# Six of the seven second products of a Winograd pair: w2's columns as weights, tokens moving, sums turned on VectorE

## The chip, the core and the metric

The program runs on one core of a Trainium2 chip. TensorE (PE in the profile; its weight loads are PEld) multiplies, VectorE (DVE) and ScalarE (ACT) do elementwise work, GpSimd (POOL) and SyncE (SP) mostly start DMAs. Matmuls write PSUM, of which this kernel uses eight banks of 128 partitions x 512 floats. The metric is the device time of one execution in microseconds, the median of several runs.

## The reference, cut to what matters

One transformer block for 2048 tokens of width 512: a modulated layer norm, linear attention and a residual, then a second modulated layer norm, a dense layer to 1792 features, Mish, and a dense layer back to 512, again with a gate and a residual:

```python
h = _layernorm(x) * (1 + cb) + sb
sp = softplus(h @ w1 + b1);  act = (h @ w1 + b1) * tanh(sp)      # Mish, [2048, 1792]
x = x + gb * (act @ w2)                                           # w2: [1792, 512]
```

All is float32. The kernel carries each operand as two float32r parts (hi, lo) and takes hi x hi, hi x lo and lo x hi: three matmuls stand for one product (`mm3`, L72).

## The kernel before

**Blocks and tiles.** The tokens are four blocks of 512; the 1792 features are 14 tiles of 128 (`NF`), taken in seven pairs (`G`). Blocks 0 and 1 go through the feed-forward layer first: the first dense layer as a Winograd scheme of seven products per pair (`product`, `pair_begin`, `pair_early`, `pair_middle`, `pair_end`, L1127 to L1184), the second one plainly (`d_unit`, L1107), with the activations as weights, 128 tokens at a time, and 512 columns of w2 moving.

**The last two blocks** (2 and 3; from L1305) use a Winograd scheme for the second layer too. Its left matrix has the two blocks as rows and the two feature tiles of a pair as columns (a11, a12 of block 2, a21, a22 of block 3); its right matrix has the two feature tiles as rows and the two halves of w2's 512 columns as columns. Per pair there are seven products, each summed over the seven pairs in PSUM: m1 = a11 b11, m2 = a12 b21, m4 = a22 t4, m5 = s1 t1, m6 = s2 t2, m7 = s3 t3, m3 = s4 b22. The left sums are s1 = a21 + a22, s2 = s1 - a11, s3 = a11 - a21 (in the code a21 - a11, taken with a sign), s4 = a12 - s2. The results are m1 + m2, m1 + m6 + m5 + m3, m1 + m6 + m7 - m4 and m1 + m6 + m7 + m5, each plus a residual that lies in DRAM (`x1d`).

**One unit** is one product of one pair: `seventh` (L1321) with four tiles of 128 tokens as weights, three matmuls each, 256 columns of w2's part moving: 12 matmuls. The two PSUM banks of a product hold two token tiles of 256 columns each. m1 and m2 are run between the products of the first layer (`e_unit`, `gap`, L1333 and L1416; for the last pair after the second unit of m4), then come m4, m6, m7, m5 as 28 units in this order (L1435 to L1461). m3 (L1463 to L1471) comes last and by token tiles: 21 matmuls of 256 columns, an add, a store, four times.

**Order of the work.** It is written out by hand: each engine runs its instructions in the order in which the code emits them. Work beside TensorE's is kept in generators, which `tick` (L57) moves on by one step after each unit; `spawn` puts one in line, `spawn_idle` into a second line of which a few move on per tick. `left_sums` (L1337) makes the left sums in place, `split` makes hi on ACT and lo on DVE, `left_prep` (L1355) prepares a left operand some five units ahead. `left_trail` does it for the first five pairs during the first layer. `finish` (L1361) adds a finished product into the residual tiles `rq`, 512 elements per partition at a time, and stores them; `load_r` (L1310) loads these tiles from DRAM on SP.

**Buffers.** Tiles of 2 KB per partition come from one pool of `SLOTS` = 97; whoever needs a tile takes the one that has been free longest and waits for its last reader. A DMA that loads weights (`load_wb` L763, `load_wt` L1388, on POOL) or residuals (SP) so waits for a tile.

**w2's preparation** (`w2_job`, L702) runs during blocks 0 and 1: each 128 rows of w2 are multiplied with the gate on DVE, split, and written to DRAM; `w2_sums` (L730) makes the four right sums of a pair.

Of the kernel before, what the change touches and what calls it, by code (L numbers as in the profile page):

```python
# [13 lines left out]
P = 128  # L14
S = 2048
D = 512
# [1 line left out]
NB = S // 512  # L18
NF = F // P
LAG = 3  # L20
SLOTS = 97
EPS = 1e-5
TINY = 1e-6

# [1 line left out]
def block_kernel(ctx: ExitStack, tc: tile.TileContext, x, wqkv, wo, w1, b1t, w2, c, wmodt, out):  # L26
# [668 lines left out]

    w2r = {}

    def load_w2(f):
        w2r[f] = sb(f"w2r_{f}")
        sp.dma_start(w2r[f], w2[P * f:P * (f + 1), :])  # L700

    def w2_job(f, wait=2):  # L702
        if f not in w2r:
            load_w2(f)
            for _ in range(wait):
                yield
        t = w2r[f]
        dve.tensor_tensor(t, t, bc["gb"], op=ALU.mult)
        yield
        yield from split(f"w2_{f}", t, w2s, f)  # L710
        yield
        g, n = f // 2, f % 2
        if n == 0:
            if g in SUMS_KEPT:
                w2f[g] = drp.tile([P, 2, D], F32, name=f"w2f_{g}")
            for i in range(2):
                w2d[g, i] = drp.tile([P, 2, D], F32R, name=f"w2d_{g}_{i}")
        for i in range(2):
            pool.dma_start(w2d[g, i][:, n, :], w2s[f][i])
        if g in SUMS_KEPT:  # L720
            pool.dma_start(w2f[g][:, n, :], t)
        elif g < KEPT and n:
            for _ in range(1 if g else 6):
                yield
            yield from w2_sums(g)
# [4 lines left out]
    def w2_sums(g):  # L730

        if g in SUMS_KEPT:
            r = [sb(f"w2p_{g}_{i}") for i in range(2)]
            for i in range(2):
                sp.dma_start(r[i], w2f[g][:, i, :])
        else:
            r = [w2r[2 * g + i] for i in range(2)]
        yield
        yield
        h = D // 2  # L740
        b11, b12, b21, b22 = [v[:, c:c + h] for v in r for c in (0, h)]
        ta, tb = [sb(f"t{n}_{g}") for n in (12, 34)]
        t1, t2, t3, t4 = ta[:, 0:h], ta[:, h:D], tb[:, 0:h], tb[:, h:D]
# [158 lines left out]
    def o_post(p, b, t):  # L902
        r = xt["r", b, t]
        dve.tensor_tensor(r, p, r, op=ALU.add)  # L904
        if b >= 2:
            yield
            if t % 2 == 0:
                x1d[b, t // 2] = drp.tile([P, 2, D], F32, name=f"x1d_{b}_{t // 2}")
            pool.dma_start(x1d[b, t // 2][:, t % 2, :], r)

    def o_unit(b, t, tag="acc"):
        p = ps(tag, f"o_{b}_{t}")
# [206 lines left out]

    ub = {}  # L1120
# [186 lines left out]
    banks, rq, U = {}, {}, {}  # L1307
    width[0] = 3

    def load_r(n, c):  # L1310

        for i in range(2):
            rq[n, c, i] = sb(f"rq_{n}_{c}_{i}", F32, (P, 2, D // 2))
            sp.dma_start(rq[n, c, i], x1d[L + n, i][:, :, D // 2 * c:D // 2 * (c + 1)])

    def store(n, c, i, lo=0, hi=2):
        r0 = 512 * (L + n) + 2 * P * i
        sp.dma_start(out[r0 + P * lo:r0 + P * hi, D // 2 * c:D // 2 * (c + 1)].rearrange("(t p) c -> p t c", p=P),
                     rq[n, c, i][:, lo:hi, :])

    def seventh(name, tag, left, right, n, last):  # L1321

        if n == 0:
            banks[name] = [ps(tag, f"{name}_{i}") for i in range(2)]
# [5 lines left out]
    def bank(name, i):  # L1330
        return banks[name][i].rearrange("p (t c) -> p t c", t=2)

    def e_unit(c, n):  # L1333
        g = pairs[n]
# [2 lines left out]
    def left_sums(g, fine=False):  # L1337

        a11, a12, a21, a22 = ua[2 * g], ua[2 * g + 1], ub[2 * g], ub[2 * g + 1]
        yield from split(f"l4_{g}", a22, left, ("m4", g))  # L1340
        for n, (d, u, v, op) in enumerate(((a22, a21, a22, ALU.add), (a21, a11, a21, ALU.subtract),
                                           (a11, a22, a11, ALU.subtract), (a12, a12, a11, ALU.subtract))):
            if fine or n == 2:
                yield
            dve.tensor_tensor(d, u, v, op=op)
        sums_of[g] = {"m5": a22, "m7": a21, "m6": a11, "m3": a12}

    left, sums_of = {}, {}

# [3 lines left out]
        yield from left_sums(g, True)  # L1353

    def left_prep(name, g):  # L1355
        return left_sums(g) if name == "m4" else split(f"l_{name}_{g}", sums_of[g][name], left, (name, g))

    def add_r(n, c, i, v, op=ALU.add):
        dve.tensor_tensor(rq[n, c, i], rq[n, c, i], v, op=op)

    def finish(name):  # L1361
        for i in range(2):
            p = bank(name, i)
            if name == "m2":
                U[i] = sb(f"U_{i}", F32, (P, 2, D // 2))
                act.activation(U[i], bank("m1", i), AF.Copy)
                add_r(0, 0, i, bank("m1", i))
                add_r(0, 0, i, p)
                store(0, 0, i)
            if name == "m4":  # L1370
                add_r(1, 0, i, p, ALU.subtract)
            if name == "m6":
                dve.tensor_tensor(U[i], U[i], p, op=ALU.add)
                add_r(0, 1, i, U[i])
            if name == "m7":
                dve.tensor_tensor(U[i], U[i], p, op=ALU.add)
                add_r(1, 0, i, U[i])
                store(1, 0, i)
                add_r(1, 1, i, U[i])
            if name == "m5":  # L1380
                add_r(0, 1, i, p)
                add_r(1, 1, i, p)
                store(1, 1, i)
            yield

    wt, SUM = {}, {"m5": 0, "m6": 1, "m7": 2, "m4": 3}

# [14 lines left out]
    for n, g in enumerate(pairs):  # L1402
# [9 lines left out]
            load_r(0, 0)  # L1412
        if n == 6:
            for m in pairs[:5]:
                load_wt("m4", m)
        def gap(c, m):  # L1416
            def unit():
                e_unit(c, m)
# [21 lines left out]
    load_r(1, 0)  # L1440
    tags = {"m4": "h", "m6": "acc", "m7": "acc", "m5": "h"}
    for k, (name, n) in enumerate(units[:4 * G]):
        for _ in range(2 if k in (6, 10, 14, 18) else 1):
            if ahead_of:
                nm, m = ahead_of.pop(0)
                spawn(left_prep(nm, pairs[m]))
        for _ in range(2 if k < 3 else 1):
            if loads:
                nm, m = loads.pop(0)
                load_wt(nm, pairs[m])  # L1450
        if k in (3, 8):
            load_r(k // 8, 1)
        seventh(name, tags[name], left.pop((name, pairs[n])), wt.pop((name, pairs[n])), n, G - 1)
        if n == G - 1:
            spawn(finish(name))
        tick()
        if k == 1:
            e_unit(0, G - 1)
            e_unit(1, G - 1)
            spawn(finish("m2"))  # L1460
            tick()  # L1461

    last = [ps("acc", f"m3_{t}") for t in range(4)]  # L1463
    for t in range(4):
        p = last[t][:, 0:D // 2]
# [3 lines left out]
        v = rq[0, 1, t // 2][:, t % 2, :]  # L1469
        dve.tensor_tensor(v, v, p, op=ALU.add)  # L1470
        store(0, 1, t // 2, t % 2, t % 2 + 1)  # L1471


# [30 lines left out]
```

## Time and profile before

| what | us |
| --- | --- |
| runs | 489.94, 490.17, 492.12 (median 490.17) |
| the profiled execution, its own time | 490.62 |
| its span in the profile | 488.9 |
| TensorE busy in it | 482.3 (99%), 2574 matmuls |
| VectorE, ScalarE, GpSimd busy | 397.8, 303.9, 120.5 |
| first layer of the last two blocks, with m1 and m2 | 348.19 to 432.21 |
| m4, the last of m1 and m2, m6, m7, m5 | 432.21 to 475.44 |
| m3 and the end | 475.44 to 488.9 |

In the order of time, a row has the start in us, the duration in us, the engine, the line, the operation, what it writes and from what, the shapes, and in brackets how long the engine sat idle before it and what ended that. Matmuls overlap: the time that one takes in a stream is the distance of two starts, not the duration. In the rows of a stretch, each engine has its busy time and its instructions in brackets; behind them stand the granted clock of TensorE, the busy share of the DMA engines and GB/s. In rows of a tile or a line, the durations are least/median/most in ns. Rows of DMA issues give KB of each and us to landing. Tile names have their numbers left out: `m` is the PSUM tile of any of m1 to m7, `p_a` and `p_s` those of the first layer.

### The profile page before, as it was taken

How to read it: one execution, taken by the hardware profiler on the slowest of the kernel's cores; microseconds unless marked ns; L12 is line 12 of the kernel's file. 1: busy time of each engine (PE TensorE's matmuls, PEld its weight loads, DVE VectorE, ACT ScalarE, POOL GpSimd, SP SyncE). 2: the span in 40 equal slices, each digit the busy share in tenths (PEclk: the TensorE clock that was granted, in tenths of full speed). 3: DMA queues.
4: the chain of work that ended last, by engine and by line, in shares of the span. 5: the costliest groups of instructions: out<-in, count | busy, mean ns of one | idle time of the engine just before them, and what ended most of it. 6: DMA issues, size and time to landing. Idle time of an engine off the chain costs nothing.

```text
span 488.9 us, 7482 instructions
## 1 busy us (share of the span) xinstructions
PE 482.3 (99%) x2574; PEld 404.5 (83%) x2574; DVE 397.8 (81%) x775; ACT 303.9 (62%) x549; POOL 120.5 (25%) x200
## 2 busy tenths in 40 slices
PE   8999999999999999999999999999999999999997
PEld 6688877768887888888888888888888888899997
DVE  6999898998999799988998763798444898869772
ACT  6787469755754979557887655783065576668100
POOL 3673121000022123113435115141101100445200
PEclk9999999999999999999999999999999999999999
DMA  8904859644884428168759359994733304688612
GB/s 303 379 8 88 193 109 275 198 130 117 263 203 110 108 68 255 65 195 279 241 164 252 120 138 293 370 341 108 215 87 86 88 0 130 156 214 233 154 44 86
DMA packets 67392, 83.88 MB, mean 172 GB/s; under 512 B 6001, under 2 KB 41337, under 8 KB 67354
## 3 DMA queue, kind: packets, MB, share of 16 engines
q1 hardware_dynamic: 44424, 48.65, 33.1%
q0 software_dynamic: 22784, 34.49, 26.5%
q8 instruction: 20, 0.33, 0.3%
q10 hardware_dynamic: 146, 0.26, 0.1%
q14 instruction: 18, 0.15, 0.1%
HBM read 56.89 MB, written 24.38 MB: 166 GB/s over the span
## 4 chain that ended last, share of the span: by engine, by line
PE 84%; DMA 6%; DVE 6%; ACT 1%; SPq 1%; POOL 1%; issue 1%; DVEq 0%
PE p_a L1133 20%; PE p_s L1133 8%; PE oacc L76 5%; PE oacc L75 5%; PE oacc L74 5%; PE m L76 5%; PE m L75 5%; PE m L74 5%; PE o L74 3%; PE o L76 3%; PE o L75 3%; PE pq_a L376 3%; DMA sq_x<-wide_x 3%; DMA wm<-in_wmodt_dram 2%; PE pq L74 2%; PE pq L76 1%
## 5 line engine op out<-in xcount | busy, mean ns | idle before, releaser
L1143 ACT ACTIVATE u<-p_a 128x512 f32<-128x512 f32 x14 | 8.4, 598 | 29.2 <-PE p_a L1133 29.2
L767 POOL DMA_DIRECT2D wb<-w2d x14 | 9.8, 705 | 67.2 <-PE p_a L1133 30.6
L1138 DVE TENSOR_TENSOR cb<-p_s,u 128x512 f32<-128x512 f32 x28 | 19.1, 686 | 7.7 <-ACT u L1174 7.6
L199 POOL TENSOR_TENSOR rs_n<-rs_n,half 128x1 f32<-128x1 f32 x16 | 10.0, 627 | 57.1 <-DVE rs_n L225 44.3
L1125 ACT ACTIVATE ub<-cb,b1c 128x512 f32<-128x512 f32 x28 | 20.0, 718 | 5.6 <-DVE cb L1138 5.5
L1168 ACT ACTIVATE u<-p_a 128x512 f32<-128x512 f32 x12 | 7.2, 598 | 25.8 <-PE p_a L1133 25.8
L1400 POOL DMA_DIRECT2D wt_m<-w2t x20 | 14.0, 702 | 29.1 <-PE m L76 20.9
L880 POOL DMA_DIRECT2D rden_d<-rden x2 | 1.5, 736 | 60.3 <-DVE rden L878 60.3
L1102 ACT ACTIVATE u<-p_a,b1c 128x512 f32<-128x512 f32 x14 | 9.6, 688 | 9.6 <-PE p_a L1133 9.6
L773 POOL DMA_DIRECT2D w2b<-w2d x20 | 10.6, 543 | 20.0 <-PE oacc L76 12.4
L1138 DVE TENSOR_TENSOR c<-p_a,u 128x512 f32<-128x512 f32 x14 | 9.5, 685 | 6.4 <-PE p_a L1133 5.2
L1174 ACT ACTIVATE u<-p_a 128x512 f32<-128x512 f32 x14 | 8.3, 595 | 8.7 <-PE p_a L1133 8.3
L1117 DVE TENSOR_TENSOR r<-oacc,r 128x512 f32<-128x512 f32 x8 | 5.5, 691 | 8.8 <-PE oacc L76 8.8
L290 DVE SCALAR_TENSOR_TENSOR ku<-e_k,relu_k 128x512 f32<-128x512 f32 x16 | 11.3, 703 | 1.5 <-ACT relu_k L288 1.5
L290 DVE SCALAR_TENSOR_TENSOR q<-e_q,relu_q 128x512 f32<-128x512 f32 x16 | 10.6, 683 | 1.2 <-ACT relu_q L288 1.2
L199 POOL TENSOR_TENSOR rs_x<-rs_x,half 128x1 f32<-128x1 f32 (+1 forms) x10 | 7.8, 786 | 15.0 <-DVE rs_x L194 14.2
L190 DVE BATCH_NORM_STATS2 st_x<-x 128x6 f32<-128x512 f32 x13 | 8.8, 676 | 3.1 <-DMA x<-in_x_dram 3.1
L904 DVE TENSOR_TENSOR r<-o,r 128x512 f32<-128x512 f32 x16 | 10.8, 675 | 0.6 <-PE o L76 0.6
L287 ACT ACTIVATE e_k<-pk 128x512 f32<-128x512 f32 x16 | 9.4, 586 | 2.7 <-PE pk L76 2.7
L892 DVE SCALAR_TENSOR_TENSOR q<-q,rd 128x512 f32<-128x512 f32 x16 | 10.4, 683 | 0.2 <-DMA rd<-rden_d 0.2
L299 POOL DMA_DIRECT2D ku<-ku x8 | 7.2, 939 | 13.4 <-DVE ku L290 13.4
L175 DVE SCALAR_TENSOR_TENSOR wm<-wm,sc_row 128x512 f32<-128x512 f32 x16 | 10.4, 680 | 0.0
(1588 smaller groups left out, 1981.7 us busy)
## 6 DMA issues: line engine op xcount, KB each, us to landing
wm<-in_wmodt_dram SPq DMA_DIRECT2D x24, 256.0 KB, 5.4
w1p<-in_w_dram SPq DMA_DIRECT2D x24, 256.0 KB, 5.3
w2b<-w2d POOLq DMA_DIRECT2D x20, 256.0 KB, 7.9
wt_m<-w2t POOLq DMA_DIRECT2D x20, 256.0 KB, 4.5
r<-in_x_dram SPq DMA_DIRECT2D x16, 256.0 KB, 2.8
x<-in_x_dram SPq DMA_DIRECT2D x15, 256.0 KB, 4.8
w2r<-in_w_dram SPq DMA_DIRECT2D x14, 256.0 KB, 5.7
wb<-w2d POOLq DMA_DIRECT2D x14, 256.0 KB, 3.6
```

Of the source, the lines that this page charges most:

```text
L74: pe.matmul(o, st[0], mv[0], start=start, stop=False)
L75: pe.matmul(o, st[0], mv[1], start=False, stop=False)
L76: pe.matmul(o, st[1], mv[0], start=False, stop=stop)
L199: pool.tensor_tensor(y, y, half[:, lo:hi], op=ALU.pow)
L290: dve.scalar_tensor_tensor(dst, e, 1.0, r, op0=ALU.min, op1=ALU.add)
L376: pe.matmul(p, l, r, start=onto is None and c == 0 and i == 0, stop=c == 1 and i == 2, skip_group_check=onto is not None)
L773: pool.dma_start(w2s[f][i], w2d[f // 2, i][:, f % 2, :])
L904: dve.tensor_tensor(r, p, r, op=ALU.add)
L1125: act.activation(u, p, AF.Mish, bias=b1c[:, f:f + 1])
L1133: pe.matmul(p, st, mv, start=onto is None and c == 0 and i == 0, stop=c == 1 and i == 2, skip_group_check=onto is not None)
L1138: dve.tensor_tensor(out, p, u, op=ALU.add)
L1400: pool.dma_start(v, w2t[g][:, :, SUM[name], :])
```

## The change

For all products but m3, the roles are turned. The weights are now 128 columns of w2's part (its 256 columns in two groups q), and the left operand's 512 tokens move: two groups, three matmuls each, 6 matmuls of 512 columns per unit. A product's two banks now hold w2's columns on the partitions and 512 tokens in a row. m3 keeps its form.

So the sums come out turned. `total` adds two parts into a tile `y` and turns it in blocks of 32 x 32 on VectorE into one large tile `z` (two groups, two results at a time). For that the first half of w2's columns is kept in another order: column 64a + 32q + c lies at 128q + 32a + c, so that a partition of `z` has 64 columns, 256 bytes, that lie together in the output. `w2_job` writes this order when it multiplies with the gate, in two instructions per tile and into a new tile; `w2_sums` reads the second half in the same order; blocks 0 and 1 undo it in their last add, also in two instructions.

The residual of a result is loaded in the same pieces (`load_r`: four DMAs of 32 partitions, 16 x 256 bytes each) into one buffer `Y`, added in one instruction of 1024 elements (`result`), and stored in such pieces (`store`), on SP or ACT. One result, m1 + m6 + m5 of block 2's second half, goes to DRAM (`c12`) and is loaded back as rows (`rn`), and m3 is added to it. The order of the products becomes m6, m5, m7, m4, m3; s1 gets a tile of its own, since a22 is needed until m4. The pool has 95 tiles.

```diff
-SLOTS = 97
+SLOTS = 95
...
-        t = w2r[f]
-        dve.tensor_tensor(t, t, bc["gb"], op=ALU.mult)
+        v, t = w2r[f], sb(f"w2g_{f}")
+        for h, d in enumerate(halves(t)):
+            c = slice(D // 2 * h, D // 2 * (h + 1))
+            s_ = [u[:, c] if h else u[:, c].rearrange("p (a q c) -> p a q c", a=4, q=2) for u in (v, bc["gb"])]
+            dve.tensor_tensor(d, *s_, op=ALU.mult)
+        w2r[f] = t
...
-                dve.tensor_tensor(v, oacc[t], v, op=ALU.add)
+                h0 = v[:, 0:D // 2].rearrange("p (a q c) -> p a q c", a=4, q=2)
+                dve.tensor_tensor(h0, halves(oacc[t])[0], h0, op=ALU.add)
+                dve.tensor_tensor(v[:, D // 2:D], oacc[t][:, D // 2:D], v[:, D // 2:D], op=ALU.add)
...
+    def in_squares(d, c):
+        return [bass.AP(tensor=d.tensor, offset=d.offset + H * c + 64 * a, ap=[[D, 32], [32 * D, 16], [1, 64]])
+                for a in range(4)]
     def load_r(n, c):
-        for i in range(2):
-            rq[n, c, i] = sb(f"rq_{n}_{c}_{i}", F32, (P, 2, D // 2))
-            sp.dma_start(rq[n, c, i], x1d[L + n, i][:, :, D // 2 * c:D // 2 * (c + 1)])
+        y = rq[n, c] = big.tile([P, 16, 64], F32, tag="Y", name=f"rq_{n}_{c}", bufs=1)
+        for a, d in enumerate(in_squares(x1d[L + n], c)):
+            sp.dma_start(y[32 * a:32 * (a + 1)], d)
+    def store(n, c, y, d=None, eng=sp):
+        if d is None:
+            d = out[512 * (L + n):512 * (L + n + 1), :]
+        for a, v in enumerate(in_squares(d, c)):
+            eng.dma_start(v, y[32 * a:32 * (a + 1)])
     def seventh(name, tag, left, right, n, last):
...
-        for t in range(4):
-            h = t % 2
-            mm3(banks[name][t // 2][:, D // 2 * h:D // 2 * (h + 1)], [a[:, P * t:P * (t + 1)] for a in left], right,
-                n == 0 and h == 0, n == last and h == 1)
+        for q in range(2):
+            mm3(banks[name][q], [w[:, P * q:P * (q + 1)] for w in right], left, n == 0, n == last)
...
+    def total(n, c, q, u, p, op=ALU.add):
+        y = sb(f"y_{n}_{c}_{q}")
+        dve.tensor_tensor(y, u, p, op=op)
+        if not Z:
+            Z.append(big.tile([P, 16, 4, 32], F32, tag="W", name="z", bufs=1))
+        dve.transpose(Z[0][:, :, 2 * (n ^ c) + q, :], y.rearrange("p (m c) -> p m c", c=32))
+    def result(n, c):
+        z = Z[0][:, :, 2 * (n ^ c):2 * (n ^ c) + 2, :].rearrange("p m q c -> p m (q c)")
+        dve.tensor_tensor(z, z, rq.pop((n, c)), op=ALU.add)
+        if (n, c) != (0, 1):
+            store(n, c, z, eng=sp if c == n else act)
+            return
+        d = drp.tile([512, D], F32, name="c12")
+        store(n, c, z, d)
+        for i in range(2):
+            rn[i] = sb(f"rn_{i}", F32, (P, 2, H))
+            sp.dma_start(rn[i], bass.AP(tensor=d.tensor, offset=d.offset + 2 * P * D * i + H,
+                                        ap=[[D, P], [P * D, 2], [1, H]]))
...
-    names = ["m4", "m6", "m7", "m5", "m3"]
+    names = ["m6", "m5", "m7", "m4", "m3"]
...
-        if k in (3, 8):
-            load_r(k // 8, 1)
+        if k in (2, 10, 17):
+            load_r(*{2: (0, 1), 10: (1, 1), 17: (1, 0)}[k])
```

`finish` now does, for q = 0 and 1 one tick apart: after m2 a copy of m1 to `U` on ACT and the total U + m2; after m6 U + m6; after m5 a copy of m5 to `V` on ACT and the total U + m5; after m7 U + m7 and the total U + V; after m4 the total U - m4. `result` follows one tick later (three after m2).

More of the change, by code (lines that the diff above doesn't have):

```diff
@@ L906, in o_post @@
             yield
-            if t % 2 == 0:
-                x1d[b, t // 2] = drp.tile([P, 2, D], F32, name=f"x1d_{b}_{t // 2}")
-            pool.dma_start(x1d[b, t // 2][:, t % 2, :], r)
+            if t == 0:
+                x1d[b] = drp.tile([4, P, D], F32, name=f"x1d_{b}")
+            pool.dma_start(x1d[b][t], r)
     def o_unit(b, t, tag="acc"):
@@ L1339, in left_sums @@
         a11, a12, a21, a22 = ua[2 * g], ua[2 * g + 1], ub[2 * g], ub[2 * g + 1]
-        yield from split(f"l4_{g}", a22, left, ("m4", g))
-        for n, (d, u, v, op) in enumerate(((a22, a21, a22, ALU.add), (a21, a11, a21, ALU.subtract),
-                                           (a11, a22, a11, ALU.subtract), (a12, a12, a11, ALU.subtract))):
+        s1 = sb(f"ls_{g}")
+        for n, (d, u, v, op) in enumerate(((s1, a21, a22, ALU.add), (a21, a11, a21, ALU.subtract),
+                                           (a11, s1, a11, ALU.subtract), (a12, a12, a11, ALU.subtract))):
             if fine or n == 2:
@@ L1345, in left_sums @@
             dve.tensor_tensor(d, u, v, op=op)
-        sums_of[g] = {"m5": a22, "m7": a21, "m6": a11, "m3": a12}
+        sums_of[g] = {"m4": a22, "m5": s1, "m7": a21, "m6": a11, "m3": a12}
+        yield from split(f"l_m6_{g}", a11, left, ("m6", g))
     left, sums_of = {}, {}
@@ L1361, in finish @@
     def finish(name):
-        for i in range(2):
-            p = bank(name, i)
+        for q in range(2):
+            p = banks[name][q]
             if name == "m2":
[L1365 to L1369, printed above, removed]
-            if name == "m4":
[L1371 to L1383, printed above, removed]
-            yield
+                U[q] = sb(f"U_{q}")
+                act.activation(U[q], banks["m1"][q], AF.Copy)
+                total(0, 0, q, U[q], p)
+            if name == "m6":
+                dve.tensor_tensor(U[q], U[q], p, op=ALU.add)
+            if name == "m5":
+                V[q] = sb(f"V_{q}")
+                act.activation(V[q], p, AF.Copy)
+                total(0, 1, q, U[q], p)
+            if name == "m7":
+                dve.tensor_tensor(U[q], U[q], p, op=ALU.add)
+                total(1, 1, q, U[q], V[q])
+            if name == "m4":
+                total(1, 0, q, U[q], p, ALU.subtract)
+            yield
@@ L1386, in block_kernel @@
+        if name != "m6":
+            if name == "m2":
+                yield
+                yield
+            result(*{"m2": (0, 0), "m5": (0, 1), "m7": (1, 1), "m4": (1, 0)}[name])
     wt, SUM = {}, {"m5": 0, "m6": 1, "m7": 2, "m4": 3}
@@ L1468, in block_kernel @@
         tick()
-        v = rq[0, 1, t // 2][:, t % 2, :]
+        v = rn[t // 2][:, t % 2, :]
         dve.tensor_tensor(v, v, p, op=ALU.add)
-        store(0, 1, t // 2, t % 2, t % 2 + 1)
+        r0 = 512 * L + P * t
+        sp.dma_start(out[r0:r0 + P, H:D], v)
 def kernel(**inputs):
```

26 lines of the change are left out of this document (11 added, 15 removed).

## The prediction

> **What bounds the kernel now.** I read the page first: the busy lines.
>
> ```profile
> PE 482.3 (99%) x2574; PEld 404.5 (83%) x2574; DVE 397.8 (81%) x775; ACT 303.9 (62%) x549; POOL 120.5 (25%) x200
> ```
>
> PE is busy 99% of the span, and each of its 2574 matmuls has a weight load of its own. So time can be won only by fewer or cheaper matmuls. The next view is busy time by stage: blocks 0 and 1 (one piece of them), then the first products of the last two blocks with m1 and m2 between them, then the second products, then m3 and the end.
>
> ```profile
> 240.00:290.00 50.00, 50.00 (x222) 41.39 (x221) 43.88 (x91) 35.69 (x67) 15.20 (x27) 1.00 0.62 183
> 348.19:432.21 84.02, 84.02 (x439) 72.23 (x438) 58.05 (x106) 50.46 (x87) 14.41 (x21) 1.00 0.45 119
> 432.21:475.44 43.23, 43.23 (x361) 43.13 (x360) 35.59 (x57) 17.84 (x34) 12.60 (x22) 1.00 0.59 151
> 475.44:488.90 13.46, 10.36 (x87) 10.15 (x85) 3.76 (x8) 0.00 (x0) 0.00 (x0) 0.98 0.24 80
> ```
>
> PE has no gap from 240 to 475 us, at a granted clock of 1.00. DVE has 6.1 of 50 us free in the first row and 7.6 of 43.2 in the third.
>
> What does one matmul cost? The chain of waits has a row for twelve matmuls of 512 columns back to back, and the order of time shows those of 256.
>
> ```profile
> 370.17 2.72 PE p_a L1133 x12
> ```
>
> ```profile
> 363.01 0.28 PE L74 MATMUL m<-wb,a_10h 128*128 128x256 f32 x1
> 363.12 0.28 PE L75 MATMUL m<-wb,a_10h 128*128 128x256 f32 x1
> 363.24 0.28 PE L76 MATMUL m<-wb,a_10l 128*128 128x256 f32 x1
> ...
> 364.44 0.40 PE L1133 MATMUL p_a<-t_0h,s_6h 128*128 128x512 f32 x1
> ...
> 365.83 0.28 PE L74 MATMUL m<-wb,a_12h 128*128 128x256 f32 x1
> ```
>
> From start to start, 512 columns take 2.72/12 = 0.2267 us and 256 columns 0.12 us (363.12 to 363.24). Per column that is (226.7 - 120)/256 = 0.417 ns, and 226.7 - 512 x 0.417 = 13 ns are left that each matmul costs whatever its width. Two narrow ones cost 0.24 us, one wide one 0.2267. This difference of 13 ns is all that the change can win on PE.
>
> **What it removes on PE.** Six products of 7 pairs are 42 units. A unit was 12 matmuls of 256 columns and becomes 6 of 512: 252 matmuls fewer, the same columns streamed. Twelve units (m1 and m2 of six pairs) stand between 512-column products. One there takes 364.44 - 363.01 = 1.43 us, and the product behind it 365.83 - 364.44 = 1.39, against 2.72/2 = 1.36 for a product among its like; so 1.43 + 1.39 - 2 x 1.36 = 0.10 us each, 1.2 us in all. The other 30 units run in one piece:
>
> ```profile
> 432.21 0.28 PE L74 MATMUL m<-wt_m,l_5h 128*128 128x256 f32 x1
> ...
> 445.28 0.28 PE L75 MATMUL m<-wt_m,l_m_5h 128*128 128x256 f32 x1
> 445.46 0.39 PE L76 MATMUL m<-wt_m,l_m_5l 128*128 128x256 f32 x1
> 445.68 0.28 PE L74 MATMUL m<-wt_m,l_m_5h 128*128 128x256 f32 x1
> ...
> 475.56 0.28 PE L74 MATMUL m<-wt_m,l_m_5h 128*128 128x256 f32 x1
> ...
> 485.52 0.28 PE L76 MATMUL m<-wt_m,l_m_4l 128*128 128x256 f32 x1
> 485.83 0.42 DVE L1470 TENSOR_TENSOR rq<-rq,m 128x256 f32<-128x256 f32 x1 [2.10 <-PE m L76]
> ```
>
> 475.56 - 432.21 = 43.35 us; 30 x 1.36 = 40.8. That wins 2.55 us, of which 0.16 is the one stall of before, at 445.46, where the second product waited for its first left operand (0.18 + 0.22 instead of twice 0.12). Together 3.75 us. The 84 matmuls of m3 (475.56 to 485.52) stay. I take the 0.2267 us for the new ones because the 512-column products load a fresh 128 x 128 weight for each matmul too.
>
> The Trainium skill, TensorE: Matmul & The Clock Gate, section Back-to-back issue gap, gives N/2.4 + 2.5 ns for a warm array, so 109 and 216 ns, and by it the change would win only 252 x 2.5 ns = 0.6 us. The slope agrees with the trace (0.417 ns is 1/2.4), the fixed part doesn't: the rows have 13 ns, and they decide.
>
> **What it puts on DVE.** Rows for the pieces:
>
> ```profile
> L239 DVE STREAM_TRANSPOSE wide_n<-r x8: 699/702/712, 240.8 to 288.3; 128x512 f32<-128x512 f32 x8
> L793 DVE TENSOR_TENSOR s<-w1p x12: 381/415/419, 105.6 to 406.4; 128x256 f32<-128x256 f32 x12
> ```
>
> ```profile
> 433.05 0.68 DVE L1138 TENSOR_TENSOR cb<-p_s,u 128x512 f32<-128x512 f32 x1
> ...
> 449.52 0.68 DVE L88 TENSOR_TENSOR l_m_4l<-u,l_m_4h 128x512 fp32r<-128x512 f32 x1
> 450.13 0.68 DVE L88 TENSOR_TENSOR l_m_5l<-ub,l_m_5h 128x512 fp32r<-128x512 f32 x1
> ```
>
> Finishing the products was 20 adds of 512 elements; it becomes 12 such adds, 8 transposes at 0.70 and 4 adds of 1024 elements. The last are not in the trace: from 0.42 us at 256 and 0.68 at 512 elements, about 1.2 us each; at least 0.68, at most twice 0.70. The transposes stand in for the eight adds saved, so the 4 x 1.2 = 5 us are what comes on top, in a stage where DVE has 7.6 us free: hidden, if nothing is late at one place. That place is the start of m5. DVE is behind there, because the sums of the last two pairs come after the last results. I run its order by hand. The first unit starts at 432.21 - 1.2 = 431.0. DVE ends the last result (433.05 before) at 432.6, then does eight sums at 0.61 to 0.72 and the low half for pair 3, to 438.4; a copy on ACT and the total, 439.8; transpose, 440.5; the low half for pair 4, 441.1 (PE wants it at 431.0 + 8 x 1.36 = 441.9); total and transpose, 442.5; the first low half of m5, 443.1. PE wants that one with its second matmul of m5, at 431.0 + 9 x 1.36 + 0.2 = 443.5. The margin is 0.4 us. Each further low half takes 0.61 us (449.52 to 450.13) against 1.36 of a unit, and the first wide add of a residual (1.2 us) stands before the third of them. If nothing hid these steps they would cost the totals' 4 x 0.7; I put down 0.4 us of stall, between -0.16 (no stall any more) and 1.5.
>
> In blocks 0 and 1 the scaling of w2 splits into two adds' worth: 14 x (0.84 - 0.68) = 2.3 us, and the last adds of both blocks 8 x 0.16 = 1.3, beside PE, with 6.1 of 50 us free there. Were the 32-element runs slower by half, it would be 28 x 0.2 more, still under what is free. I put 0.1 us.
>
> **Queues and buffers.** Weight loads on POOL wait for free tiles, not for data:
>
> ```profile
> 417.49 3.49 POOL L1400 DMA_DIRECT2D wt_m<-w2t  x5 [13.45 <-PE m L76]
> 424.85 1.40 POOL L1400 DMA_DIRECT2D wt_m<-w2t  x2 [3.87 <-DVE c L1138]
> 426.91 2.09 POOL L1400 DMA_DIRECT2D wt_m<-w2t  x3 [0.66 <-ACT u L1102]
> ```
>
> ```profile
> rq<-x1d SPq DMA_DIRECT2D x8, 256.0 KB, 4.4
> wt_m<-w2t POOLq DMA_DIRECT2D x20, 256.0 KB, 4.5
> sq_x<-wide_x SPq DMA_DIRECT2D x8, 256.0 KB, 4.9
> wm<-in_wmodt_dram SPq DMA_DIRECT2D x24, 256.0 KB, 5.4
> w1p<-in_w_dram SPq DMA_DIRECT2D x24, 256.0 KB, 5.3
> ```
>
> Counted in the code from first to last use, at most 91 of 97 tiles are live when the first five weights of the second products are given out. The change keeps one more tile for each of five pairs (the separate sum), needs two fewer for the residual and has 95: about one left instead of six, so a load gets its tile some five releases later. The next five loads, of the last two rows, show when those releases come: 424.85 to 429. Even then the first weights land by 424.85 + 0.7 + 4.5 = 430.1, before 431.0, and the third is wanted only behind two units and those of m1 and m2, at 436.5. I put 0, between 0 and 4 (the rival below). In blocks 0 and 1, and where the keys' products take 93 tiles, fewer tiles shift the waits in the same way; PE had no gap there, and I put 0.
>
> ```profile
> L1314 SPq DMA_DIRECT2D rq<-x1d x8: 530/560/1519, 403.4 to 448.2; - x8
> ```
>
> SP: each load of the residual now has four issues of 0.56 us instead of two, and waits for the result before it, since there is one buffer. Behind it on SP wait the store of that same result, the parked sum's stores and reloads, and the next load. The tightest is the last: m7 ends at 431.4 + 23 x 1.36 = 462.7 (0.4 us of stall counted), twice an add, a total and a transpose (2.1 us) and the wide add end at 468.1, four issues and 4.4 us to landing at 474.7. DVE wants it behind m3's first add, at 475.4. On POOL nothing new is queued. The last pieces go out on ACT, which has 0.00 us of work after 475.44. So these cost 0.
>
> **Sum.** 490.62 us is the profiled execution's own time (span 488.9). 490.62 - 3.75 + 0.4 + 0.1 = 487.4; that execution is 0.45 above the median of the runs, 490.17, so against the median 490.17 - 3.25 = **486.9 us**.
>
> **Rivals.** (1) DVE late at m5: the totals and transposes of m2 come one behind the other (1.4 us twice) with 0.4 us of margin. For it: 445.46 shows that DVE is late just there now. Against: it catches up 0.75 us a unit. With 1.5 us of stall: 488.0.
>
> (2) Slower than before: pieces of 256 bytes are slow to land. m3 begins at 475.56 - 3.4 = 472.2; its first add starts 2.8 us later and ends at 475.4, the wide add at 476.6, four issues at 479. The rest ends at 485.83 - 3.4 + 0.42 + 2.65 = 485.5 (2.65 us is what lay behind the last add), so the pieces decide from 6.5 us to landing on. Pieces of 512 bytes took 4.9 us (the squares) and 5.3 (w1), those of 2 KB 5.4 (the modulation weights): size made no difference. If pieces of 256 bytes cost double, 9.8 us, the chained loads are late too: from the second result at 457.2 to 469.2, from the third at 470.4 to 482.4, and the last store lands at 483.6 + 2.2 + 9.8 = 495.6, 10 us behind 485.5: 497. The Trainium skill, DMA: Bandwidth & Descriptors, section Specifications, states that below 512 B a transfer becomes a read-modify-write. No row here has such a transfer of weight, so the trace neither bears that out nor excludes it.
>
> (3) Tiles: with ten releases more instead of five, the first weights come out after 426.91 + 2.09 = 429.0 and land after 429.0 + 0.9 + 0.7 + 4.5 = 435, 4 us late: 490.9. Against it are the five of the count.
>
> (4) The change does its work and wins nothing on PE: a wide matmul with these weights takes 0.24 us, because the 13 ns belong to loading and not to the instruction. Then 490.17 + 0.5 = 490.7. Against it: the 512-column products before and after load weights as large for each matmul and hold 0.2267.
>
> **Chances.** The forecast 0.60, (1) 0.17, (2) 0.08, (3) 0.07, (4) 0.05, and 0.03 that no stall is left and the gain is 3.9 or more (486.3). What differs by under 0.5% (2.45 us) can't be told from no change. Nearly all of the forecast's case and a part of (1) lie below 487.7: faster 0.69. The rest of (1), (4), most of (3) and the milder forms of (2) are within: 0.24. Slower, full (2) and worse forms of (3): 0.07. The likeliest case alone spans 486.1 to 487.8; the range that leaves 2 in 10 out goes from 486.0 to 489.6.
>
> **What would show it.** In the changed profile: 252 matmuls fewer (2322); 0.227 us from start to start in m1 to m7 and 1.36 us a unit; m3's first matmul near 472 instead of 475.56; DVE some 5 us busier between; PE gaps only at the start of m5. I am wrong if the wide matmuls come every 0.24 us, if PE waits for weight loads around 431, or if the chain of waits ends in a DMA of the pieces instead of m3's last add and store.

## The result, and the profile after

The changed kernel takes 487.06 us (median of six runs, 486.50 to 487.60) beside 490.39 us for the kernel before on the same chip (489.94 to 492.47). The ratio is 0.9922, with a 95% interval from 0.9900 to 0.9945: 3.3 us, 0.8%. The forecast was 486.9. Its profiled execution took 487.57 us, with a span of 485.9.

The page of the changed kernel: its busy line, and its line on DMA packets.

```profile
PE 478.1 (98%) x2322; PEld 390.8 (80%) x2322; DVE 403.9 (83%) x801; ACT 305.6 (63%) x551; POOL 120.2 (25%) x200
...
DMA packets 81023, 84.90 MB, mean 175 GB/s; under 512 B 22705, under 2 KB 54969, under 8 KB 80986
```

There are 252 matmuls fewer and 4.2 us less of TensorE. VectorE has 6.1 us more. Busy time by stage, in the changed kernel's own stages (a piece of blocks 0 and 1; first products with m1 and m2; m6, m5, m7, m4; m3 and the end):

```profile
240.00:290.00 50.00, 50.00 (x222) 41.40 (x221) 44.61 (x100) 35.91 (x67) 15.16 (x27) 1.00 0.60 180
...
347.00:431.00 84.00, 84.00 (x371) 69.23 (x370) 59.55 (x111) 50.33 (x86) 13.93 (x20) 1.00 0.45 113
431.00:472.00 41.00, 41.00 (x182) 33.97 (x181) 38.91 (x60) 19.37 (x37) 13.10 (x23) 1.00 0.83 185
472.00:485.90 13.90, 10.51 (x86) 10.22 (x85) 5.31 (x9) 0.00 (x0) 0.00 (x0) 1.00 0.58 120
```

TensorE is still full, at a granted clock of 1.00. VectorE is busy for 38.9 of the 41 us of the second products; before it was 35.6 of 43.2. In the order of time: the first of m1, the first of the 30 units, the start of m5, the first of m3, and the end.

```profile
363.23 0.39 PE L74 MATMUL m<-a_10h,wb 128*128 128x512 f32 x1
...
431.47 0.39 PE L74 MATMUL m<-l_m_5h,wt_m 128*128 128x512 f32 x1
...
443.71 0.39 PE L74 MATMUL m<-l_m_5h,wt_m 128*128 128x512 f32 x1
443.94 0.39 PE L75 MATMUL m<-l_m_5l,wt_m 128*128 128x512 f32 x1
...
472.27 0.28 PE L74 MATMUL m<-wt_m,l_m_5h 128*128 128x256 f32 x1
...
482.54 0.42 DVE L1504 TENSOR_TENSOR rn<-rn,m 128x256 f32<-128x256 f32 x1 [2.09 <-PE m L76]
```

472.27 - 431.47 = 40.80 us, which is 30 x 1.36 to the hundredth: no stall is left in the long piece. Beside the marks of before:

| mark | before | after | difference |
| --- | --- | --- | --- |
| first matmul with `wq_2h` (attention) | 118.11 | 118.34 | +0.23 |
| first matmul of m1 | 363.01 | 363.23 | +0.22 |
| first of the 30 units | 432.21 | 431.47 | -0.74 |
| first matmul of m3 | 475.56 | 472.27 | -3.29 |
| last add | 485.83 | 482.54 | -3.29 |
| end of the span | 488.9 | 485.9 | -3.0 |

Between the first m1 and the first m3 the kernel wins 3.51 us (112.55 to 109.04), of the 3.75 us that the sum promised. The rest is lost at three places: 0.24 us between 363 and 431, 0.29 us behind the last add (2.94 us instead of 2.65), and 0.2 us at the start. The 0.2 us at the start can't be laid to the change: starts vary by more than that between executions. Two kernels that share all code up to 430 us, the changed one and one of the experiments below (three more turns), in the order of time:

```profile
23.64 0.50 PE L74 MATMUL gacc<-pk_0h,xn_0h 128*128 128x512 f32 x1 [0.17 <-ACT pk_0h L82]
...
118.34 0.50 PE L376 MATMUL pq_a<-qt_3h,wq_2h 128*128 128x512 f32 x1
```

```profile
22.79 0.51 PE L74 MATMUL gacc<-pk_0h,xn_0h 128*128 128x512 f32 x1
...
117.83 0.50 PE L376 MATMUL pq_a<-qt_3h,wq_2h 128*128 128x512 f32 x1
```

Over the changed kernel and the runs below that keep its 95 tiles, this last matmul starts between 117.68 and 118.52 us. So what follows is compared by **the stretch**, from the first matmul of m1 to the first of m3. It holds all 42 changed units and nothing of the start or the end.

| kernel | stretch, us | median time, us |
| --- | --- | --- |
| before | 112.55 | 490.39 to 490.68, by call |
| changed | 109.04 | 487.06 |
| all 42 units in halves of 256 columns | 112.40 | 490.66 |
| the 14 units of m1 and m2 in halves | 110.19 | 488.77 |
| in quarters of 128 | 164.47 | 542.74 (two runs) |
| in 320 and 192 | 117.10 | 495.13 (one run) |
| three more turns on VectorE | 110.92 | 488.68 |
| 91 tiles; 87 tiles | 109.02; 109.02 | 490.79; 494.91 (one run each) |
| pieces of 1 KB | 109.02 | 486.80 |
| first split of the left operands later | 108.80 | 486.37 |
| that, all stores on SP | 108.80 | 486.84 |
| that, last store on the last semaphore | 108.80 | 486.72 |

### The profile page after: what moved, and what is told of

It is laid out like the page before. It is cut to its first block, busy times and chain, and to the rows that moved or that the text cites. A ratio compares the mean times of both kernels' runs of the same rounds, so it can differ in the third digit from the quotient of the medians.

```text
span 485.9 us, 7068 instructions
## 1 busy us (share of the span) xinstructions
PE 478.1 (98%) x2322; PEld 390.8 (80%) x2322; DVE 403.9 (83%) x801; ACT 305.6 (63%) x551; POOL 120.2 (25%) x200
## 4 chain that ended last, share of the span: by engine, by line
PE 83%; DMA 6%; DVE 6%; SPq 2%; ACT 1%; POOL 1%; issue 0%; DVEq 0%; ACTq 0%
PE p_a L1144 20%; PE p_s L1144 8%; PE oacc L75 5%; PE oacc L74 5%; PE oacc L76 5%; PE m L76 5%; PE m L74 5%; PE m L75 5%; PE o L74 3%; PE o L76 3%; PE o L75 3%; DMA sq_x<-wide_x 3%; DMA wm<-in_wmodt_dram 2%; PE pq_a L376 2%; PE pq L74 2%; PE pq L76 1%
## 5 line engine op out<-in xcount | busy, mean ns | idle before, releaser
L1127 DVE TENSOR_TENSOR r<-oacc,r 128x256 f32<-128x256 f32 x8 | 3.4, 425 | 8.8 <-PE oacc L76 8.8
```

## The experiments

**Theory: the width of the matmuls is the whole gain.** Rival: the new order of the sums and of VectorE's work made it. The test keeps roles, sums, turns, pieces and order, and halves the width alone.

```diff
-            mm3(banks[name][q], [w[:, P * q:P * (q + 1)] for w in right], left, n == 0, n == last)
+            for j in range(2):
+                ts = slice(256 * j, 256 * (j + 1))
+                mm3(banks[name][q][:, ts], [w[:, P * q:P * (q + 1)] for w in right], [a[:, ts] for a in left],
+                    n == 0 and j == 0, n == last and j == 1)
```

> The changed kernel with all else kept (roles, sums, transposes, pieces, order), but each product of 512 moving columns is issued as two of 256 with the same weights. Theory (a fixed part of 13 ns per matmul is the whole gain): a unit goes back from 1.36 to 1.44 us, 42 units x 12 x 13 ns / 2 = 3.3 us more; the 0.2 us wait at 404 us may go with it. Time 490.0 to 490.5 us, span about 489.1. Rival (most of the gain came from the new order of the sums, or from lighter DVE work at the hand-overs): the time stays under 488.5 us.

490.66 us (490.08 to 491.28), span 489.2; against before the ratio is 0.9998 (0.9985 to 1.001). The long piece in the order of time:

```profile
432.44 0.28 PE L74 MATMUL m<-l_m_5h,wt_m 128*128 128x256 f32 x1
432.55 0.28 PE L75 MATMUL m<-l_m_5l,wt_m 128*128 128x256 f32 x1
432.67 0.28 PE L76 MATMUL m<-l_m_5h,wt_m 128*128 128x256 f32 x1
...
475.63 0.28 PE L74 MATMUL m<-wt_m,l_m_5h 128*128 128x256 f32 x1
```

475.63 - 432.44 = 43.19 us = 30 x 1.44. The whole gain is gone, and all that was rebuilt around it (turns, pieces, the order) is by itself neither worth nor costs more than the interval's 0.7 us. The time lies 0.16 us above the 490.0 to 490.5 expected. Each half has a weight load of its own here (2574 of each again), so the run shows what a matmul together with its load costs, and not which of the two holds the 13 ns. Only the 14 units of m1 and m2 in halves, the same loop with `k` in place of 2:

```diff
+        k = 2 if name in ("m1", "m2") else 1
```

> The changed kernel with only the 14 units of m1 and m2 issued as halves of 256 columns, the other 28 wide. Theory (each of the 12 that stand between first-layer products costs 0.10 us, the two in one piece 0.08; the 0.2 us wait at 404 goes as the units get longer): first m3 matmul 1.1 us later than in the changed kernel, less about 0.1 to 0.2; time 488.0 us. Rival (the wide form pays only in the long piece): time under 487.3 us.

The stretch is 1.15 us longer, as expected. The time, 488.77 us (median of four runs, 488.26 to 489.07), is 0.8 above what I wrote. The profiled execution comes to its first m1 at 363.56, 0.33 us later than the changed kernel's; where the other runs lost time isn't known. The wide form pays at both places, in about the shares of the sum.

**How far the 13 ns reach.** The prediction had the fixed part "whatever its width". Four matmuls of 128 columns for one of 512:

> The same with four matmuls of 128 columns in place of each of 512, each with its own weight load. Theory (fixed part of 13 ns whatever the width): 0.0667 us per matmul, a unit of 24 takes 1.60 us, 42 x 0.24 = 10 us more: 497 us. Rival A (below some width the weight load of about 0.19 us in the rows sets the pace): a unit of 24 x 0.19 = 4.56 us, 134 us more: 621 us. Between the two: the load sets the pace at some shorter time of its own, which the spacing of the matmuls then shows.

542.74 us. Order of time:

```profile
450.06 0.28 PE L75 MATMUL m<-l_m_6l,wt_m 128*128 128x128 f32 x1
450.18 0.28 PE L76 MATMUL m<-l_m_6h,wt_m 128*128 128x128 f32 x1
450.29 0.27 PE L74 MATMUL m<-l_m_6h,wt_m 128*128 128x128 f32 x1
```

And the group of its weight loads for one operand (count, busy time, mean ns):

```profile
L74 PEld LDWEIGHTS m<-l_m_6h,wt_m 128*128 128x128 f32 x32 | 6.1, 192 | 0.0
```

The 30 units in one piece, 446.99 to 527.34, hold 720 matmuls: (527.34 - 446.99)/720 = 0.1116 us from start to start, neither the 0.067 that 13 ns and 128 columns would give nor the 0.19 that a load's row shows. 42 x 24 x (0.1116 - 0.0567) = 55.3 us; the stretch is 55.4 longer. The Trainium skill, TensorE: Matmul & The Clock Gate, section LDWEIGHTS (loading the stationary operand), gives a weight load its columns over 1.2 GHz, 107 ns for 128 columns; the spacing is near that, the row of 192 ns isn't. To see if 0.111 us is a floor, one matmul above it and one below; the edit is against the halves, and its `mm3` takes the columns `ts`:

```diff
-            for j in range(2):
-                ts = slice(256 * j, 256 * (j + 1))
+            for ts in (slice(0, 320), slice(320, 512)):
```

> The changed kernel with each product of 512 columns in two matmuls of 320 and 192 columns. If the time of one is 13 ns and 0.417 ns a column whatever the width: 0.147 and 0.093 us, together 0.240, as two halves of 256: span 489.2. If the spacing can't fall below the 0.111 us that the matmuls of 128 columns showed: 0.147 and 0.111, 0.258 together, a unit of 1.55 us, 42 x 0.19 = 7.8 us more than the changed kernel's 485.9: span 493.7.

One run, span 493.4. The stretch is 8.06 us longer, against 7.8 for the floor and 3.4 without one.

```profile
427.35 0.25 PE L74 MATMUL m<-a_6h,wb 128*128 128x192 f32 x1
427.44 0.27 PE L75 MATMUL m<-a_6l,wb 128*128 128x192 f32 x1
427.55 0.28 PE L76 MATMUL m<-a_6h,wb 128*128 128x192 f32 x1
427.67 0.41 PE L1144 MATMUL p_a<-t_0h,s_4h 128*128 128x512 f32 x1
```

The first of the three comes at its own pace (0.09 us); the next two come every 0.11 to 0.12. So in a row of like matmuls with weight loads of their own, each takes the larger of 0.11 us and 13 ns + 0.417 ns a column: that fits the 128, 192, 256 and 512 columns measured here. 256 columns, at 0.120, are just above the floor. That the load is what sets the floor fits these numbers; no run here has loads of another width.

**VectorE's margin at m5**, the first rival. Three more turns of the first result, 2.1 us:

```diff
-        dve.transpose(Z[0][:, :, 2 * (n ^ c) + q, :], y.rearrange("p (m c) -> p m c", c=32))
+        for _ in range(3 - q if (n, c) == (0, 0) else 1):
+            dve.transpose(Z[0][:, :, 2 * (n ^ c) + q, :], y.rearrange("p (m c) -> p m c", c=32))
```

> The changed kernel with three more transposes of the first result (the same two sums are turned three times and twice in place of once each), so VectorE has 3 x 0.71 = 2.1 us more to do between m2's end and the low half of m5's first left operand, which now is done 0.5 us before TensorE wants it. Theory (a narrow margin, after which each us of VectorE is a us of TensorE): TensorE waits about 1.6 us at the start of m5, time 488.6 us, span 487.5. Rival (VectorE catches up from its idle time before m5 or the stretch after it hides the wait): no wait over 0.3 us, time as the changed kernel's 487.06.

488.68 us (488.46 to 489.03), stretch 1.88 us longer. VectorE and, behind it, TensorE:

```profile
439.67 2.20 DVE L1382 STREAM_TRANSPOSE z<-y 128x512 f32<-128x512 f32 x3
441.80 0.65 DVE L88 TENSOR_TENSOR l_m_4l<-u,l_m_4h 128x512 fp32r<-128x512 f32 x1
...
444.46 0.65 DVE L88 TENSOR_TENSOR l_m_5l<-ls,l_m_5h 128x512 fp32r<-128x512 f32 x1
```

```profile
442.50 0.50 PE L75 MATMUL m<-l_m_4l,t_4h 128*128 128x512 f32 x1 [0.30 <-DVE l_m_4l L88]
...
445.16 0.50 PE L75 MATMUL m<-l_m_5l,wt_m 128*128 128x512 f32 x1 [1.00 <-DVE l_m_5l L88]
```

In the changed kernel `l_m_5l` is done 0.5 us before it is wanted, at 443.94:

```profile
442.76 0.65 DVE L88 TENSOR_TENSOR l_m_5l<-ls,l_m_5h 128x512 fp32r<-128x512 f32 x1
...
443.93 1.22 DVE L1385 TENSOR_TENSOR z<-z,rq 128x1024 f32<-128x1024 f32 x1
```

The three turns put 2.2 us on VectorE and cost 1.88. TensorE waits at two places, not at m5 alone: the steps to 442.50 and 445.16 take 0.69 and 1.40 us instead of 0.23, and the step behind each takes 0.34. That is 0.46 + 1.17 + 2 x 0.11 = 1.85 us. So all that goes beyond the 0.5 us of margin ends up in the kernel's time. Nothing hides it later.

**Tiles**, the third rival, with 95 made 87 and then 91:

> The changed kernel with 87 shared tiles of 2 KB instead of 95, eight fewer. Theory (by the count of live tiles, at most 91 in the last two blocks and 93 in the keys' stage, the 95 of the changed kernel are no limit; four fewer than the last blocks hold must show): waits of some tenths of a us each appear in the last blocks and in the keys' stage, span 486.5 to 492. Rival (tiles come free long before they are wanted, so that the count says nothing of time): span within 0.4 us of the changed kernel's 485.9.

> The changed kernel with 91 shared tiles instead of 95, halfway to the 87 that gave 493.1 us of span with waits at 152, 241, 256 and 260 us. Theory by the count (at most 93 live tiles in the keys' stage, 91 in the last two blocks): small waits ahead of 160 us at most, span 485.5 to 486.5. Rival (the waits grow with every tile taken away, from 95 on): half of the 7.2 us, span 489.5.

Spans 493.1, above the range written, and 489.1 (one run each): with four tiles fewer 3.2 us are lost, with eight 7.2. So my count, by which 91 would nearly do, was wrong, and the rival by which the loss grows with the tiles taken was near. But the stretch is 109.02 us in both. What TensorE waits for between 120 and 472 us (us in total, times, longest), with 87 tiles and with 91; the changed kernel has no row there:

```profile
PE p_s L1144 <- DVE cb L1149: 4.8, 3, 2.3
PE o L76 <- DVE qs_2l L88: 0.9, 1, 0.9
```

```profile
PE p_s L1144 <- DVE cb L1149: 2.3, 2, 1.2
```

With 91 tiles these waits end at 242 and 263 us, where blocks 0 and 1 run and w2 is prepared. VectorE in front of the first, with 91 tiles and then in the changed kernel:

```profile
235.57 1.29 DVE L88 TENSOR_TENSOR t_1l<-t,t_1h 128x512 fp32r<-128x512 f32 x2 [1.61 <-PE oacc L75]
```

```profile
234.00 1.29 DVE L88 TENSOR_TENSOR t_1l<-t,t_1h 128x512 fp32r<-128x512 f32 x2 [0.34 <-ACT t_1h L82]
```

A low half that needs only its high half now waits until TensorE has read something unrelated, which fits a wait for a tile. The other part of this question, the kernel before with 95 tiles instead of 97:

```diff
-SLOTS = 97
+SLOTS = 95
```

> The kernel before with 95 shared tiles instead of 97, the one part of the change that bears on all stages. Theory (tiles are no limit at 95): the time of before, 490.3 to 490.9 us, span 488.6 to 489.4, first m3 matmul 475.4 to 475.8 us, as far as the start of the program doesn't move. It is also a second look at the end: if the 2.65 us from the last sum to the end belong to the old code, they come again; if they vary from run to run, 2.9 may come. Rival (two tiles fewer add waits, which the change paid): time over 491.2 us.

490.83 us, ratio 1.0007 (0.9997 to 1.0016): two tiles fewer cost that kernel nothing that shows (at most 0.8 us by the interval).

**Pieces of 256 bytes**, the second rival. Loads and stores of the results in whole half rows of 1 KB:

```diff
-        return [bass.AP(tensor=d.tensor, offset=d.offset + H * c + 64 * a, ap=[[D, 32], [32 * D, 16], [1, 64]])
+        return [bass.AP(tensor=d.tensor, offset=d.offset + H * c + 128 * a * D, ap=[[4 * D, 32], [D, 4], [1, H]])
...
-            Z.append(big.tile([P, 16, 4, 32], F32, tag="W", name="z", bufs=1))
+            Z.append(big.tile([P, 2, 16, 2, 32], F32, tag="W", name="z", bufs=1))
...
```

> The transfers of the residual and the results of the last two blocks in pieces of 1 KB (whole half rows) instead of 256 bytes; the same bytes, the same number of issues, but values land in other places of the output. Theory (256-byte pieces cost nothing that ends up on the path): time within 0.3 us of the changed kernel's 487.06, span 485.6 to 486.0; packets under 512 B fall back to about 6,000. Rival (pieces delay the last landing, and give the 0.29 us lost after the last sum): the stretch from the last m3 sum to the end shrinks from 2.94 to 2.65 us and the residual and result transfers land in clearly under 3.4 and 4.4 us.

This kernel leaves values in other places of the output, so only its time counts. 486.80 us (486.67 to 486.97), stretch 109.02, end 2.92 us: no difference but a shorter start. Its page, and the landings of the residual's loads (least/median/most), then the same row of the changed kernel:

```profile
DMA packets 68735, 84.90 MB, mean 175 GB/s; under 512 B 6321, under 2 KB 42681, under 8 KB 68698
```

```profile
DMA to landing us min/median/max: 2.7/2.9/4.0
```

```profile
DMA to landing us min/median/max: 2.7/3.4/5.1
```

A load in small pieces lands 0.5 us later in the median, far from twice as late, and nobody waits for it.

**The 0.24 us between 363 and 431.** Nearly all of it is lost at one place. The changed kernel there, ScalarE and TensorE in the order of time:

```profile
401.93 0.62 ACT L82 ACTIVATE l_m_0h<-u 128x512 fp32r<-128x512 f32 x1
...
402.45 1.14 ACT L82 ACTIVATE t_3h<-t 128x512 fp32r<-128x512 f32 x2
...
403.50 0.58 ACT L1185 ACTIVATE u<-p_a 128x512 f32<-128x512 f32 x1
...
404.12 0.50 PE L1144 MATMUL p_a<-t_0h,a_2h 128*128 128x512 f32 x1
...
404.46 0.39 PE L1144 MATMUL p_a<-t_0l,a_2h 128*128 128x512 f32 x1
```

The bank `p_a` is written again at 404.12, and ScalarE empties it only then, because three copies stand ahead. One of them, `l_m_0h`, is new at this place: the first split made by `left_trail` is now m6's, which needs the sums first. One more `yield` moves it:

```diff
     def left_trail(g):
         yield
         yield
+        yield
```

> The changed kernel with the sums and the first split of the left operands of the pairs done one step of the work list later. Theory (the 0.2 us wait of TensorE at 404.1 us is the first copy of an m6 left operand, 0.62 us, which now stands on ScalarE ahead of the eviction of the bank that the next product writes): the wait at 404 goes, unless the copy of another pair lands ahead of another eviction; span 485.7 us, time about 486.9. Rival (the shorter m1 unit alone uncovers the eviction): the wait stays, span 485.9.

```profile
402.65 0.60 ACT L1185 ACTIVATE u<-p_a 128x512 f32<-128x512 f32 x1
403.14 0.62 ACT L82 ACTIVATE l_m_0h<-u 128x512 fp32r<-128x512 f32 x1
...
403.81 0.39 PE L1144 MATMUL p_a<-t_0h,a_2h 128*128 128x512 f32 x1
404.04 0.39 PE L1144 MATMUL p_a<-t_0l,a_2h 128*128 128x512 f32 x1
```

The stretch is 108.80 us: the 0.24 are back, and 112.55 - 108.80 = 3.75. The time, 486.37 us (486.25 to 487.08), can't be told from the changed kernel's. The edit puts the copies of `t_3` behind the eviction too; of the three, `l_m_0h` alone did not stand there before the change. It takes the shorter unit as well: with the 14 units of m1 and m2 in halves, the same three copies stand ahead, and `p_a` is empty (404.42 + 0.57) before it is wanted:

```profile
404.42 0.57 ACT L1185 ACTIVATE u<-p_a 128x512 f32<-128x512 f32 x1
...
405.13 0.41 PE L1144 MATMUL p_a<-t_0h,a_2h 128*128 128x512 f32 x1
```

**The 0.29 us at the end.** The profiles of the changed kernel and of the runs above have 2.87 to 2.94 us from the end of the last add to the end of the span, also with pieces of 1 KB, and the run with quarters 541.1 - 537.66 - 0.42 = 3.02; the kernel before has 2.65, and with 95 tiles 489.1 - 486.01 - 0.42 = 2.67:

```profile
486.01 0.42 DVE L1470 TENSOR_TENSOR rq<-rq,m 128x256 f32<-128x256 f32 x1 [2.10 <-PE m L76]
```

The DMA engines' busy tenths behind the last add, before (40 slices of 0.069 us) and after (0.074 us):

```profile
DMA  0000000000003899984100000004000000000000
```

```profile
DMA  0000000000026999840000000000000000000000
```

The block of nines is the last store. It is over after 1.3 to 1.4 us in both, so the loss lies behind it. The first theory was ScalarE's queue, new in this stage; the edit comes on top of the later split:

```diff
-            store(n, c, z, eng=sp if c == n else act)
+            store(n, c, z)
```

> The left operands' first split one step later (as in the run of that edit alone, 486.37 us, span 485.4), and besides the fourth result stored by the same queue as all others instead of ScalarE's. Theory (the 0.25 us more between the last transfer and the end is the program's end waiting on more transfers of a second queue): the stretch from the last m3 sum's end to the end of the span falls from 2.90 to 2.65 us, span about 485.2. Rival (the end is longer by the number of transfers or by something else): it stays at 2.90, or the four issues delay m3's stores and it grows.

```profile
481.68 0.42 DVE L1505 TENSOR_TENSOR rn<-rn,m 128x256 f32<-128x256 f32 x1 [2.10 <-PE m L76]
```

It was wrong: 485.0 - 481.68 - 0.42 = 2.90 us again. The second was the order in which the program's end waits. The edit, again on top of the later split, loads the first residual by eight transfers instead of four, so that the last store falls on another of the eight semaphores:

```diff
-            sp.dma_start(y[32 * a:32 * (a + 1)], d)
+            if (n, c) != (0, 0):
+                sp.dma_start(y[32 * a:32 * (a + 1)], d)
+                continue
+            for k in range(2):
+                half = bass.AP(tensor=d.tensor, offset=d.offset + 256 * D * k, ap=[[D, 32], [32 * D, 8], [1, 64]])
+                sp.dma_start(y[32 * a:32 * (a + 1), 8 * k:8 * (k + 1)], half)
```

> The left operands' first split one step later (that edit alone: 486.37 us, span 485.4), and the first residual, which SP asks for 60 us before it is wanted, loaded by eight transfers instead of four. The transfers signal by eight semaphores in turn, and the program's end waits for these in the order 0 to 7: in the kernel before the last store signals number 7, the last one waited for; in the changed kernel number 3, and four waits are still to be gone through after it. The four transfers more put the last store on number 7 again. Theory (these four waits are the 0.25 us by which the end is longer in every form of the changed kernel, and which neither the size of the pieces nor ScalarE's queue explained): from the last m3 sum's end to the end of the span 2.65 us instead of 2.90, span about 485.1, time 486.1 us. Rival (the end is longer by something else, as the number of transfers): 2.90 or more, span 485.4.

```profile
482.24 0.42 DVE L1510 TENSOR_TENSOR rn<-rn,m 128x256 f32<-128x256 f32 x1 [2.10 <-PE m L76]
```

485.3 - 482.24 - 0.42 = 2.64 us. The semaphore events in the traces bear the order out. In the changed kernel the last store lands at 484.70 us on number 3, and SP's waits for the other four start at 484.78, 484.84, 484.90 and 484.96. In the kernel before it lands at 487.98 on number 7, the last wait. In the run with quarters it falls on number 2, one wait more, and that run has the longest end. The time, 486.72 us (486.25 to 487.03), is again not to be told from the changed kernel's; both repairs together are 0.5 us by the traces, and the start takes as much from run to run.

## Why the prediction was right

**TensorE: right.** 0.2267 us per wide matmul, 1.36 us a unit, 40.8 us for the thirty and 0.10 for each of the other twelve all came as written. The repaired kernel's stretch shows the sum of 3.75 us to the hundredth. Rival (4) is out, as a wide matmul with these weights took 0.2267 us and not 0.24; and undoing the width alone takes the gain back, so it comes from issuing fewer matmuls with their loads. The 2.5 ns per matmul, by which the change would have won 0.6 us, stand in the Trainium skill (TensorE: Matmul & The Clock Gate, section Back-to-back issue gap) for a matmul by itself; for a stream of loads and matmuls the same section gives 131 ns at 512 columns. The prediction named only the first. Neither holds for these matmuls: the rows have 226.7 ns. The words "whatever its width" were too wide: below about 236 columns ((111.6 - 13)/0.417) the floor sets the pace. It didn't matter here, as 256 lies above.

**VectorE at m5: the place right, the term too large.** Low half done at 443.1 by hand, 443.4 in the trace, whose first unit starts 0.5 us later than put by hand; margin 0.4 by hand, 0.5 in the trace; 0.4 us of stall put down, none came. The run with more turns shows that the chosen place was indeed the narrow one and what lies behind its edge. The low half of the pair before (`l_m_4l`), which had 0.8 us by hand (441.1 and 441.9), has 1.1 in the trace (441.49 and 442.58), and with more turns it is waited for too. The wide add took 1.22 us for an estimate of 1.2, the turns 0.71 for 0.70.

**Blocks 0 and 1: right.** 0.1 us put, none found: the offset is 0.23 us at 118 and 0.22 at 363. VectorE's free 5.4 of 50 us there hide the added instructions. They are also fewer microseconds than the 3.6 put (2.3 + 1.3): from 150 to 345 us VectorE's busy time grew by 1.34 us (163.46 to 164.80). The sum went by durations, and instructions in a row overlap: four half multiplications of 0.42 us take 1.43 together.

**Queues and buffers: right in the sum, wrong in the reason.** TensorE has no wait at 431 us, and even with 87 tiles the stretch is no longer. The count of live tiles from the code looked for the narrow place in the last blocks and the keys' products; the runs show it near 242 to 263 us, where four tiles fewer already cost 3.2 us. Rival (3) did not come with 95 tiles and had the stage wrong; that 3.2 us is near its 4 us is chance. Which tiles are held there too long was not followed further.

**Pieces: right.** m3 began at 472.27 (472.2 forecast). Pieces of 256 bytes didn't cost double. What the Trainium skill (DMA: Bandwidth & Descriptors, section Specifications) states of transfers below 512 B can account, in these runs, for at most the 0.5 us to a load's landing; whether there was a read-modify-write they don't show.

**What the sum lacked.** Two losses weren't seen: the copy that moved on ScalarE, ahead of a bank that a shorter unit wants sooner (0.24 us), where I costed the new order of the splits at nothing without looking at the evictions behind it; and the end (0.29), where "2.65 us is what lay behind the last add" was carried over. For the profiled executions: 490.62 - 3.75 + 0.24 + 0.29 + 0.2 (start) = 487.6, measured 487.57; the sum of the prediction, 487.4, had 0.5 us of other losses that didn't come. So the nearness of 486.9 to 487.06 is partly that these errors cancel.

## What to carry to other kernels

When TensorE is full and each matmul loads its own weights, count matmuls: each, with its load, costs a fixed 13 ns here, so the widest moving operand wins, and below about 236 columns a floor of 0.11 us per matmul sets the pace instead. Turning a product round to get there costs work on other engines that is free only as far as the narrowest handover allows; run that handover by hand, and every instruction on ScalarE that a reordering puts in front of an eviction too. With gains under 1 us, compare stretches between two marks of the traces, since the start alone moves by as much.

## What was not expected of the hardware

- After a wait of TensorE, the step from the first matmul to the next takes 0.34 us instead of 0.23 (404.12 to 404.46, 442.50 to 442.84, 445.16 to 445.50).
- A weight load of 128 x 128 shows 0.19 us in its rows, but consecutive matmuls with loads of their own of 128 columns come every 0.1116 us: the loads overlap each other or their rows hold a wait.
- Behind the last transfer the end of the program takes 0.25 us more or less by the semaphore on which the last store falls, 0.06 us for each wait of SP still to be gone through.
- The first 24 us differ by 0.85 us (22.79 to 23.64 at the same matmul) between executions of the same code; of that, 0.5 us are left at the first matmul of m1 (362.71 and 363.23).
